# Taking the causal mask of transposed attention scores from TensorE to ScalarE and GpSimd

## The chip, the core and the metric

One NeuronCore of a Trainium2 chip runs the whole program. The metric is the device time of one execution in microseconds. The engines are named as the profile names them: PE (TensorE, matmuls and transposes; PEld is its weight load), DVE (VectorE), ACT (ScalarE), POOL (GpSimd), SP (SyncE, which issues most DMAs).

## The reference

Four layers run over x of 2048 rows and 512 columns: a spectral layer, an attention layer, and both again. The spectral layer adds to x the real part of a Fourier transform of its layernorm, as matrix products with given cosine and sine matrices. The attention layer has 32 heads of 16 columns and cuts the rows into 4 segments of 512:

```
for s in range(4):
    logits = einsum(qs, ks) * scale + mask          # scale = 16 ** -0.5
    p = softmax(logits)
    a_dot = einsum(p, vs)
    o = g * (phi(qs) @ M) / (phi(qs) @ z + 1e-6) + (1 - g) * a_dot
    M, z = M + phi(ks).T @ vs, z + sum(phi(ks))
```

The mask adds -1e9 where the key's index is greater than the query's within the segment. phi(t) is t + 1 above zero and exp(t) below; g is the sigmoid of beta, by head.

## The kernel before

The program is written as Python generators ("steps") that `place` puts into numbered slots; slots run in order, and inside a slot by a small order number. PE's instructions keep this order exactly. The instructions of the other engines are set in order by a scheduler, which looks at priorities and its own estimate of when operands are ready. PSUM has one bank for PV (`pv_bank`) and seven that every other matmul takes in turn (`bank`).

A spectral layer takes 240 slots and some lead. An attention layer takes 320: 32 units of 10 slots, each of 4 heads of one segment. The steps of a unit that begins at slot t:

- `stack` (t - 21) loads q and k of the unit from DRAM, three bf16 parts of each in 96 rows (tiles stkq, stkk).
- `natural_max` (t - 17 to t - 7): PE forms scores with queries in rows (tile nat, 10 banks a unit), DVE takes each row's maximum with the mask added (`junk`, L414, accumulator mx), and turns it into three bf16 parts of the negated maximum.
- `max_rows` (t - 5): PE transposes them (mT), ACT copies them (mt, L452) and issues a DMA that writes them as 3 more rows under q; k has ones there.
- `softmax_values` (t to t + 11): PE forms the transposed scores, keys in rows (tile sT, 99 rows, the maximum already subtracted), ACT takes Exp into tile pT, and PE multiplies with v (PV). For a key block kt only the query columns from kt * 128 on are formed. The ten banks of a unit are two `third` (blocks of 256 and 256 columns: key block 2 of two heads), four `second` (384 and 128: key blocks 1 and 3), four `first` (512: key block 0). They stand in slots t, t + 1; t + 2 to t + 5; t + 6 to t + 9. `last` (PV of all four heads, and the copy ot on ACT) stands in slot t + 11.
- `output` (t + 13): PE transposes ot (tile on), DVE divides by the softmax's sum, POOL adds the result to the memory's part in onat.

Only the first 128 columns of each block hold masked places, since there key and query come from the same 128 rows. They were masked by a second matmul into the same bank, of an identity and a constant tile mask_t:

```
T.matmul(ps[:, off : off + P], ident_b, mask_t, start=False, stop=True)
```

Beside the units run the projections (`proj`, tile pqk, for q and k of the next group; pvv for v), the layernorm of the next segment (`prep`: st, mv, r on POOL, xn), the output projection (on, oT, oh, po) and the memory (pm, pM, pkT). `proj` ends with ACT copying the bank to bf16 (parts 0), ACT making phi, DVE taking the remainder (rem), ACT rounding it (parts 1), POOL subtracting once more (parts 2, L347), and SP writing the parts to DRAM. Steps that fill a unit with matmuls go to `light` slots, which leave out two of ten: those of PV and of `output`.

Of the kernel before, what the change touches and what calls it, by code (L numbers as in the profile page):

```python
# [18 lines left out]
P = 128  # L19
# [11 lines left out]
LAST = range((NSEG - 1) * LT, NT)  # L31
EPS = 1e-5
SCALE = DH ** -0.5
MASK = -1e9 / SCALE
SLOTS = {"q": ((0, 3, 0), (1, 2, 0), (2, 1, 0)), "k": ((0, 3, 1), (0, 2, 1), (0, 1, 1))}
NSLOT = 6
KROWS = NSLOT * DH
# [8 lines left out]
def spectral_infini_kernel(  # L46
# [228 lines left out]
    def place_attention(x_in, x_out, t0, w_at, out_at, resident):  # L275
# [39 lines left out]
        def proj(s, g, n):  # L315
            ps = bank("pqk")
            for d in range(DT):
                matmul3(
                    ps,
                    lambda h: ws[n, d][:, h, g * P : (g + 1) * P],  # L320
                    lambda h: xT[s][:, h, d, :],
                    d == 0,
                    d == DT - 1,
                )
                if d + 1 < DT:
                    yield

            def phi_tile():
                if (s, g) not in phi:
                    phi[s, g] = pair("phi", "ut", 8, F32)  # L330
                return phi[s, g][:, "qk".index(n)]

            parts = sb.tile([P, 3, 512], BF16, name="parts", bufs=2)
            with_phi = (n == "q" and s > 0) or (n == "k" and s < NSEG - 1)
            late = s == 0 and g < 2
            rem = sb.tile([P, 512], F32, name="rem", bufs=1)
            A.activation(parts[:, 0], ps, AF.Copy)
            if with_phi:
                raw = sb.tile([P, 512], F32, name="praw", bufs=2)
                A.activation(raw, ps, AF.Copy if late else AF.Relu)  # L340
                if not late:
                    A.activation(phi_tile(), ps, AF.Exp)
            V.tensor_tensor(out=rem, in0=ps, in1=parts[:, 0], op=ALU.subtract)
            yield
            yield
            A.activation(parts[:, 1], rem, AF.Copy)
            G.tensor_tensor(out=parts[:, 2], in0=rem, in1=parts[:, 1], op=ALU.subtract)  # L347
            if with_phi and not late:
                V.scalar_tensor_tensor(
                    phi_tile(), phi_tile(), 1.0, raw, op0=ALU.min, op1=ALU.add  # L350
                )
            yield
            sd = dram.tile([NSLOT, P, 512], BF16, name=f"scr{n}", bufs=3)
            dst = sd.rearrange("o p s -> p o s")
            o = 0
            for a, cnt, step in SLOTS[n]:
                src = parts[:, a : a + cnt] if step else parts[:, a : a + 1].to_broadcast(
                    [P, cnt, 512]
                )
                nc.sync.dma_start(dst[:, o : o + cnt], src)  # L360
                o += cnt
            scr[s, g, n] = sd
            yield
            if with_phi and late:
                V.tensor_scalar_min(phi_tile(), raw, 0.0)
                A.activation(phi_tile(), phi_tile(), AF.Exp)
                V.scalar_tensor_tensor(
                    phi_tile(), raw, 0.0, phi_tile(), op0=ALU.max, op1=ALU.add
                )
                yield  # L370
# [21 lines left out]
        def natural_max(s, g, u):  # L392
            qs, ks = stacks[s, g, u, "q"], stacks[s, g, u, "k"]
            mx = sb.tile([P, HU, LT], F32, name="mx", bufs=2)

            def scores(*cols):
                ps = bank("nat")
                views, off = [], 0
                for h, i in cols:
                    n = (i + 1) * P  # L400
                    T.matmul(
                        ps[:, off : off + n],
                        qs[:KROWS, h, i * P : (i + 1) * P],
                        ks[:KROWS, h, :n],
                        start=True,
                        stop=True,
                    )
                    views.append((ps[:, off : off + n], mx[:, h, i : i + 1]))
                    off += n
                for src, dst in views:  # L410
                    n = src.shape[1]
                    junk = sb.tile([P, 512], BF16, name="junk", bufs=1)
                    with tc.high_priority(offset=URGENT):
                        V.tensor_tensor_reduce(  # L414
                            junk[:, :n], src, mask[:, 512 - n :], 1.0, -3e38,
                            ALU.add, ALU.max, dst,
                        )

            for h in range(HU):
                scores((h, 3))  # L420
                yield
                scores((h, 0), (h, 2))
                yield
                if h % 2:
                    scores((h - 1, 1), (h, 1))
                    yield
            parts = max_parts[((s * NG + g) * (HG // HU) + u) % 2]
            rem = sb.tile([P, HU, LT], F32, name="mrem", bufs=2)
            with tc.high_priority(offset=2 * URGENT):
                V.scalar_tensor_tensor(  # L430
                    parts[:, 0], mx, -2.0, mx, op0=ALU.mult, op1=ALU.add
                )
                for dst in rem, parts[:, 1]:
                    V.scalar_tensor_tensor(
                        dst, mx, -1.0, parts[:, 0], op0=ALU.mult, op1=ALU.subtract
                    )
                V.scalar_tensor_tensor(
                    parts[:, 2], rem, 1.0, parts[:, 1], op0=ALU.mult, op1=ALU.subtract
                )
            maxima[s, g, u] = parts  # L440
            yield
# [16 lines left out]
        def softmax_values(s, g, u):  # L458
# [3 lines left out]

            def scores(dst, *cols):
                ps = bank("sT")
                off = 0
                for h, kt in cols:
                    n = 512 - kt * P
                    T.matmul(
                        ps[:, off : off + n],
                        ks[:K, h, kt * P : (kt + 1) * P],  # L470
                        qs[:K, h, kt * P :],
                        start=True,
                        stop=False,
                    )
                    T.matmul(ps[:, off : off + P], ident_b, mask_t, start=False, stop=True)
                    off += n
                A.activation(dst, ps, AF.Exp, scale=SCALE)  # L477

            def pv(pv_bank, kt, pt, off):
                n = 512 - kt * P  # L480
# [16 lines left out]
            for h in range(HU):  # L497

                def first(h=h):
                    if h % 2 == 0:  # L500
                        p0.append(pair("pT", "wd", 8, F32))
                    scores(p0[h // 2][:, h % 2], (h, 0))

                ev(6 + h, first)
            for h in range(HU):

                def second(h=h):
                    if h % 2 == 0:
                        p1.append(pair("pT", "wd", 8, F32))
                    scores(p1[h // 2][:, h % 2], (h, 1), (h, 3))  # L510

                ev(2 + h, second)
            p2 = []
            for h in range(0, HU, 2):

                def third(h=h):
                    if h == 0:
                        p2.append(sb.tile([P, HU, 256], F32, name="pT2", tag="craw", bufs=2))
                    scores(p2[0][:, h : h + 2].rearrange("p h s -> p (h s)"), (h, 2), (h + 1, 2))

                ev(h // 2, third)

# [7 lines left out]
                A.activation(ot, pb, AF.Copy)  # L530
                outs[s, g, u] = ot

            ev(11, last)
            for t in range(12):
                for f in events.get(t, ()):
                    f()
                yield
# [183 lines left out]
            return n // USEG, n % USEG // NU, n % NU  # L721

        def light(t, n=SU):
            return [k for k in range(t, t + n) if (k - t0) % SU not in (1, 3)]

        def among(start, stop, n):
            at = light(start, stop - start)
# [8 lines left out]
            place(3, load_split(ws, (n, d), src, f"w{n}", "w", 16), [w_at(k) - 3, w_at(k)])  # L736
        for n in range(NSEG * USEG):
            t = t0 + SU * n
            place(0, softmax_values(*unit(n)), run_from(t, 12))
            place(1.9, output(*unit(n)), [t + 13])  # L740
            place(1.9, max_rows(*unit(n)), [t - 5])
            place(1, natural_max(*unit(n)), run_from(t - 17, 10), [t - 7])
            place(0.5, stack(*unit(n)), [t - 21])
# [65 lines left out]
        mids[2], out_tiles, b2, w_at(b2), lambda k: b2 + LB + 8 + k, {}  # L809
    )  # L810
    def setup():
        nonlocal ident, ident_b, mask, mask_t, same_head, gate
        with tc.issue_after(first_row[0].ins):
            ident = consts.tile([P, P], F32, name="ident")
            make_identity(nc, ident)
# [4 lines left out]
            G.affine_select(  # L820
                mask[:, 384:], mask[:, 384:], pattern=[[-1, P]], compare_op=ALU.is_ge,
                fill=MASK, base=0, channel_multiplier=1,
            )
            mask_t = consts.tile([P, P], BF16, name="mask_t")
            G.memset(mask_t, 0.0)
            G.affine_select(
                mask_t, mask_t, pattern=[[1, P]], compare_op=ALU.is_ge,
                fill=MASK, base=0, channel_multiplier=-1,
            )
            same_head = consts.tile([P, HG], F32, name="same_head")  # L830
            V.tensor_reduce(
# [14 lines left out]
            V.tensor_scalar(gate[:, 1], gate[:, 0], -1.0, 1.0, op0=ALU.mult, op1=ALU.add)  # L846
        yield

    ident = ident_b = mask = mask_t = same_head = gate = None
    place(5, setup(), [60])  # L850
    for t in sorted(slots):
        slots_done.append(t)
# [44 lines left out]
```

## Time and profile before

| | us |
|---|---|
| median of 3 runs | 1954.85 |
| lowest, highest | 1952.45, 1955.95 |
| the profiled execution | 1959.92 |
| its span | 1958.1 |
| PE busy | 1894.2 |
| DVE busy | 1104.0 |
| ACT busy | 799.2 |
| POOL busy | 214.4 |
| mask matmuls, 1024, as busy time of their own | 194.2 |

The span is the time from the first to the last instruction in the profiled execution. A row of the profile's groups names the source line, the engine, the operation, "out<-in" by tile, the shapes and the count; behind the bar stand the busy time, the mean duration in ns, and the idle time of the engine just before, with what ended it. Busy time of matmuls is modelled and neighbours overlap, so what a matmul costs PE is seen from one start to the next.

### The profile page before, as it was taken

What the parts mean: (1) busy time and instruction counts of PE and PEld (TensorE: products, weight loads), DVE (VectorE), ACT (ScalarE), POOL (GpSimd) and SP (SyncE); (2) the same over time, 40 slices, a digit from 0 to 9 for tenths busy, and PEclk for the clock granted to TensorE, in tenths of its full rate; (3) what the DMA queues carried; (4) which work ended last, traced back from release to release, by engine and by line L of the source; (5) the groups of instructions that cost most, each with busy time, mean ns of one, the idle gap of its engine ahead of it and who ended that gap; (6) DMA issues with size and microseconds to landing.
All of it is one profiled execution on the core that took longest, in us unless ns stands there. A gap on an engine that the chain in (4) does not pass through costs nothing.

```text
span 1958.1 us, 31336 instructions
## 1 busy us (share of the span) xinstructions
PE 1894.2 (97%) x11552; PEld 1393.7 (71%) x11552; DVE 1104.0 (56%) x3733; ACT 799.2 (41%) x1386; POOL 214.4 (11%) x280
## 2 busy tenths in 40 slices
PE   7999999999999999998899999999998999999998
PEld 5788888887556666665578888888875666666665
DVE  8522222255776877868744222222567768677684
ACT  3311212142655656455533121121426555565554
POOL 6100000011110111113110000000111101111110
PEclk9999999999999999999999999999999999999999
DMA  5423233345442434335234232323454434343331
GB/s 178 156 93 102 97 97 97 97 155 162 130 131 90 149 105 133 127 115 168 85 100 140 97 97 97 97 97 102 149 162 127 126 103 148 114 127 128 106 108 57
DMA packets 123113, 232.48 MB, mean 119 GB/s; under 512 B 14416, under 2 KB 63568, under 8 KB 122960
## 3 DMA queue, kind: packets, MB, share of 16 engines
q1 hardware_dynamic: 119696, 229.70, 36.4%
q8 instruction: 90, 1.47, 0.3%
q10 hardware_dynamic: 3264, 0.79, 0.2%
q14 instruction: 63, 0.52, 0.1%
HBM read 162.55 MB, written 67.11 MB: 117 GB/s over the span
## 4 chain that ended last, share of the span: by engine, by line
PE 74%; DVE 9%; issue 8%; DMA 5%; POOL 2%; ACT 1%; SPq 0%; POOLq 0%; DVEq 0%; ACTq 0%
PE u L71 33%; PE y L71 7%; PE sT L71 7%; PE pv_bank L71 5%; PE pqk L71 5%; PE nat L71 5%; DVE junk L414 4%; PE po L71 4%; PE pvv L71 3%; DMA xt<-mid 2%; DMA stkk<-scrk 2%; PE on L71 1%; DVE xn L143 1%; PE pM L71 1%; PE pm L71 1%
## 5 line engine op out<-in xcount | busy, mean ns | idle before, releaser
L71 PE MATMUL u<-chi,xh 128*128 128x512 f32 x2048 | 652.1, 392 | 14.3 <-DVE mv L124 9.0
L414 DVE CUSTOM_DVE_ANT_0 junk<-nat,mask 128x512 bf16<-128x512 f32 (+3 forms) x1024 | 498.0, 486 | 171.6 <-PE nat L71 146.8
L71 PEld LDWEIGHTS u<-chi,xh 128*128 128x128 f32 x2048 | 387.1, 189 | 97.5 <-ACT chi L83 9.0
L477 ACT ACTIVATE pT<-sT 128x512 f32<-128x512 f32 x640 | 368.6, 599 | 190.2 <-PE sT L71 180.5
L71 PE MATMUL u<-clo,xh 128*128 128x512 f32 x1024 | 401.1, 392 | 2.6 <-DVE clo L85 2.1
L85 DVE TENSOR_TENSOR clo<-craw,chi 128x1024 fp32r<-128x1024 f32 x124 | 153.0, 1234 | 423.2 <-ACT chi L83 422.8
L83 ACT ACTIVATE chi<-craw 128x1024 fp32r<-128x1024 f32 x124 | 131.3, 1059 | 533.0 <-PE u L71 523.6
L71 PE MATMUL sT<-stkq,stkk 99*128 99x256 bf16 (+3 forms) x1024 | 273.2, 307 | 7.8 <-DVE mx L414 5.9
L71 PE MATMUL nat<-stkk,stkq 96*128 96x512 bf16 (+3 forms) x1024 | 244.9, 300 | 19.5 <-DVE mx L414 7.6
L71 PEld LDWEIGHTS u<-clo,xh 128*128 128x128 f32 x1024 | 193.5, 189 | 43.2 <-DVE clo L85 3.5
L71 PEld LDWEIGHTS <-stkk 99*128 99x128 bf16 x1024 | 100.9, 99 | 140.0 <-issue 119.0
L71 PE MATMUL y<-wdt,ut 128*128 128x512 f32 x768 | 196.9, 390 | 0.0
L71 PE MATMUL sT<-mask_t,ident_b 128*128 128x128 bf16 x1024 | 194.2, 221 | 0.0
L71 PEld LDWEIGHTS y<-wdt,ut 128*128 128x128 f32 x768 | 144.1, 188 | 29.9
L71 PE MATMUL pv_bank<-pT,vt 128*17 128x256 f32 (+3 forms) x2048 | 160.2, 441 | 0.0
L128 POOL TENSOR_TENSOR r<-ve,half_neg 128x1 f32<-128x1 f32 x64 | 39.2, 614 | 920.5 <-DVE ve L126 904.9
L71 PEld LDWEIGHTS <-stkq 96*128 96x128 bf16 x1024 | 85.7, 98 | 62.3 <-issue 31.9
L71 PE MATMUL pqk<-xT,wq 128*128 128x512 f32 x384 | 125.6, 437 | 0.0
L71 PE MATMUL pqk<-xT,wk 128*128 128x512 f32 x384 | 125.4, 434 | 0.0
L71 PEld LDWEIGHTS pv_bank<-pT,vt 128*17 128x17 f32 x2048 | 61.7, 98 | 88.4 <-issue 80.4
L71 PE MATMUL pvv<-wv,xT 128*128 128x512 f32 x384 | 123.6, 430 | 0.0
L71 PE MATMUL po<-wo,oh 128*128 128x512 f32 x384 | 120.5, 429 | 1.1 <-ACT oh L83 0.7
(106 smaller groups left out, 1855.9 us busy)
## 6 DMA issues: line engine op xcount, KB each, us to landing
craw<-in_ct SPq DMA_DIRECT2D x124, 512.0 KB
stkq<-scrq SPq DMA_DIRECT2D x64, 384.0 KB
stkk<-scrk SPq DMA_DIRECT2D x64, 384.0 KB
mid<-xo SPq DMA_DIRECT2D x48, 256.0 KB
scrq<-parts SPq DMA_DIRECT2D x32, 384.0 KB
scrk<-parts SPq DMA_DIRECT2D x32, 384.0 KB
xr<-mid SPq DMA_DIRECT2D x48, 256.0 KB
xt<-mid SPq DMA_DIRECT2D x44, 256.0 KB
```

What stands on the lines that cost most here:

```text
L71: return tc.keep_in_program_order(op(*args, **kwargs))
L83: A.activation(hi, src, AF.Copy, scale=scale)
L85: lo_engine.tensor_tensor(out=lo, in0=src, in1=hi.bitcast(F32), op=ALU.subtract)
L128: G.tensor_tensor(out=r, in0=ve, in1=half_neg, op=ALU.pow)
L143: V.tensor_scalar(xn, xt, mv[:, 0:1], rr, op0=ALU.subtract, op1=ALU.mult)
L414: V.tensor_tensor_reduce(junk[:, :n], src, mask[:, 512 - n :], 1.0, -3e38, ALU.add, ALU.max, dst,)
L477: A.activation(dst, ps, AF.Exp, scale=SCALE)
```

## The change

The mask matmul and its tile mask_t go. q is negated when it is projected, so the scores in both forms are negated: the natural ones take a minimum with +1e9/scale added, and the transposed ones hold maximum minus score, which is not negative at any place that counts. On the diagonal blocks ACT applies Relu in place in PSUM, so that masked places, which may lie on the other side of zero, become zero and Exp of them stays at most 1; then Exp with -scale over the whole bank; then POOL's affine_select sets the masked half of the diagonal blocks in pT to zero. Selects are issued for two heads at once (`causal`): of `first` after heads 1 and 3, of `second` likewise for both blocks, of `third` once for four. `last` moves from slot t + 11 to t + 12, `output` from t + 13 to t + 14, and `light` leaves out slots 2 and 4 of ten where it left out 1 and 3.

```
-MASK = -1e9 / SCALE
+MASK = 1e9 / SCALE
...
-            A.activation(parts[:, 0], ps, AF.Copy)
+            sign = -1.0 if n == "q" else 1.0
+            A.activation(parts[:, 0], ps, AF.Copy, scale=sign)
...
-            V.tensor_tensor(out=rem, in0=ps, in1=parts[:, 0], op=ALU.subtract)
+            V.scalar_tensor_tensor(
+                rem, ps, sign, parts[:, 0], op0=ALU.mult, op1=ALU.subtract
+            )
...
-                            junk[:, :n], src, mask[:, 512 - n :], 1.0, -3e38,
-                            ALU.add, ALU.max, dst,
+                            junk[:, :n], src, mask[:, 512 - n :], 1.0, 3e38,
+                            ALU.add, ALU.min, dst,
...
                         start=True,
-                        stop=False,
+                        stop=True,
                     )
-                    T.matmul(ps[:, off : off + P], ident_b, mask_t, start=False, stop=True)
+                    diag.append(off // P)
                     off += n
-                A.activation(dst, ps, AF.Exp, scale=SCALE)
+                blocks = ps.rearrange("p (b c) -> p b c", c=P)
+                blocks = blocks[:, diag[0] : diag[-1] + 1 : max(1, diag[-1] - diag[0])]
+                A.activation(blocks, blocks, AF.Relu)
+                A.activation(dst, ps, AF.Exp, scale=-SCALE)
+
+            def causal(blocks):
+                G.affine_select(
+                    blocks,
+                    blocks,
+                    pattern=[[0, n] for n in blocks.shape[1:-1]] + [[1, P]],
+                    compare_op=ALU.is_ge,
+                    fill=0.0,
+                    base=0,
+                    channel_multiplier=-1,
+                )
...
+                    if h % 2:
+                        causal(p0[h // 2][:, :, :P])
...
+                    if h % 2:
+                        for c in 0, 3 * P:
+                            causal(p1[h // 2][:, :, c : c + P])
...
+                    if h == 2:
+                        causal(p2[0][:, :, :P])
...
-            ev(11, last)
-            for t in range(12):
+            ev(12, last)
+            for t in range(13):
...
-            return [k for k in range(t, t + n) if (k - t0) % SU not in (1, 3)]
+            return [k for k in range(t, t + n) if (k - t0) % SU not in (2, 4)]
...
-            place(0, softmax_values(*unit(n)), run_from(t, 12))
-            place(1.9, output(*unit(n)), [t + 13])
+            place(0, softmax_values(*unit(n)), run_from(t, 13))
+            place(1.9, output(*unit(n)), [t + 14])
```

The order of ACT's instructions (with the engines that each waits for) in the second attention layer, from the copy ot of one unit to the DMA of the maxima, before:

```order
L530 ACTIVATE ot<-pv_bank 128x512 [waits PE_49]
L346 ACTIVATE parts<-rem 128x512 [waits DVE_49]
L477 ACTIVATE pT_16940<-sT 128x512 [waits PE_49]
L477 ACTIVATE pT<-sT 128x512 [waits PE_49] x4
L452 ACTIVATE mt<-mT 48x128 [waits DMAHW0_49,PE_49]
L453 DMA stkq<-mt 3x16x128 [waits DMAHW0_49,Activation_49]
```

and after (L482 is the Relu, L483 the Exp):

```order
L482 ACTIVATE sT<-sT 128x2x128 [waits PE_49] x2
L483 ACTIVATE pT_16981<-sT 128x512 [waits Activation_49]
L349 ACTIVATE parts<-rem 128x512 [waits DVE_49]
L483 ACTIVATE pT_16981<-sT 128x512 [waits Activation_49]
L554 ACTIVATE ot<-pv_bank 128x512 [waits PE_49]
L482 ACTIVATE sT<-sT 128x2x128 [waits PE_49] x2
L483 ACTIVATE pT<-sT 128x512 [waits Activation_49] x2
L482 ACTIVATE sT<-sT 128x2x128 [waits PE_49]
L482 ACTIVATE sT<-sT 128x2x128 [waits DVE_49,PE_49]
L455 ACTIVATE mt<-mT 48x128 [waits DMAHW0_49,PE_49]
L483 ACTIVATE pT<-sT 128x512 [waits Activation_49] x2
L456 DMA stkq<-mt 3x16x128 [waits DMAHW0_49,Activation_49]
```

Each Exp now waits for its Relu instead of PE, and the Relu of the next bank often stands between the two.

PE's order in the same layer, around the transpose of the maxima mT (with what follows it in the next slot), before:

```order
L71 MATMUL mT<-ident_b,mparts_77 80x128
L71 MATMUL po<-wo,oh 128x512 x3
L71 LDWEIGHTS stkk
L71 MATMUL sT<-stkq,stkk 128x512 [waits Activation_49]
L71 LDWEIGHTS ident_b
L71 MATMUL sT<-mask_t,ident_b 128x128
L71 LDWEIGHTS stkq
L71 MATMUL nat<-stkk,stkq 128x128 [waits DVE_49]
```

and after:

```order
L71 MATMUL mT<-ident_b,mparts_77 80x128
L71 MATMUL po<-wo,oh 128x512 x3
L71 LDWEIGHTS stkk [waits PE_49]
L71 MATMUL sT<-stkq,stkk 128x512 [waits Activation_49]
L71 LDWEIGHTS stkq
L71 MATMUL nat<-stkk,stkq 128x128 [waits Activation_49]
L71 LDWEIGHTS stkq
L71 MATMUL nat<-stkk,stkq 128x384
```

The mask's weight load and matmul are gone, and nat, which waited for a bank that DVE frees, waits for one that ACT frees.

POOL's order in the same layer, one stretch of a unit or so, before it held only the subtraction, the adds and the layernorm's power; after:

```order
L486 AFFINE_SELECT pT<-pT 128x2x128 [waits PE_49,Activation_49,Pool_49]
L350 TENSOR_TENSOR parts<-rem,parts 128x512 [waits DMAHW3_49,DMAHW7_49,DMAHW2_49,Activation_49]
L486 AFFINE_SELECT pT<-pT 128x2x128 [waits PE_49,Activation_49,Pool_49]
L350 TENSOR_TENSOR parts<-rem,parts 128x512 [waits DMAHW6_49,DMAHW7_49,DMAHW5_49,Activation_49]
L486 AFFINE_SELECT pT_16981<-pT_16981 128x4x128 [waits PE_49,Activation_49]
```

Selects and subtractions alternate; each of both waits for ACT, the subtractions for earlier DMAs too.

More of the change, by code (lines that the diff above doesn't have):

```diff
@@ L464, in scores @@
                 ps = bank("sT")
-                off = 0
+                off, diag = 0, []
                 for h, kt in cols:
@@ L811, in setup @@
     def setup():
-        nonlocal ident, ident_b, mask, mask_t, same_head, gate
+        nonlocal ident, ident_b, mask, same_head, gate
         with tc.issue_after(first_row[0].ins):
@@ L822, in setup @@
                 fill=MASK, base=0, channel_multiplier=1,
[L823 to L828, printed above, removed]
             )
@@ L847, in setup @@
         yield
-    ident = ident_b = mask = mask_t = same_head = gate = None
+    ident = ident_b = mask = same_head = gate = None
     place(5, setup(), [60])
```

## The prediction

> **What bounds the kernel now.** I read the page's first part, then busy time by stretch, then one stretch instruction by instruction. The page gives
>
> ```profile
> PE 1894.2 (97%) x11552; PEld 1393.7 (71%) x11552; DVE 1104.0 (56%) x3733; ACT 799.2 (41%) x1386; POOL 214.4 (11%) x280
> ```
>
> and the view by stretch (columns: PE, weight load, DVE, ACT, POOL, granted clock, DMA share, GB/s) shows where the average hides something:
>
> ```profile
> 500.00:600.00 100.00, 92.65 (x739) 58.62 (x737) 71.52 (x301) 58.57 (x115) 11.25 (x11) 0.97 0.41 129
> ...
> 900.00:1000.00 100.00, 88.81 (x669) 55.20 (x667) 68.13 (x265) 51.70 (x94) 20.11 (x28) 0.93 0.35 116
> ...
> 1680.70:1697.50 16.80, 16.77 (x130) 11.54 (x133) 11.98 (x51) 10.94 (x22) 3.08 (x4) 1.00 0.42 134
> 1697.50:1712.00 14.50, 14.50 (x116) 9.21 (x115) 9.79 (x47) 7.10 (x14) 1.18 (x3) 1.00 0.22 70
> 1615.70:1633.20 17.50, 17.50 (x146) 13.13 (x149) 16.40 (x57) 10.60 (x21) 2.07 (x3) 1.00 0.52 167
> ```
>
> The last three are single attention units (from one PV group to the next, 64 in all): light, with a projection finished, and with a layernorm beside it. PE is busy to the last 0.03 us in all of them, so in a steady unit a PE nanosecond saved is a nanosecond of span. The first two rows hold the ramps into and out of attention, where PE idles 7 and 11 us: there it waits for others. What PE waits for elsewhere is small; its largest entry among the waits is
>
> ```profile
> PE mT L71 <- DVE mparts L437: 9.2, 5, 3.0
> ```
>
> Inside a steady unit (start, duration, instruction):
>
> ```profile
> 1708.13 0.39 PE L71 MATMUL sT<-stkq,stkk 99*128 99x512 bf16 x1
> ...
> 1709.34 0.39 PE L71 MATMUL sT<-stkq,stkk 99*128 99x512 bf16 x1
> 1709.57 0.22 PE L71 MATMUL sT<-mask_t,ident_b 128*128 128x128 bf16 x1
> 1709.63 0.38 PE L71 MATMUL nat<-stkk,stkq 96*128 96x128 bf16 x2
> 1710.55 0.28 PE L71 MATMUL sT<-stkq,stkk 99*128 99x256 bf16 x1
> 1710.68 0.22 PE L71 MATMUL sT<-mask_t,ident_b 128*128 128x128 bf16 x1
> 1710.74 0.27 PE L71 MATMUL sT<-stkq,stkk 99*128 99x256 bf16 x1
> ...
> 1711.99 0.61 PE L71 MATMUL pv_bank<-pT,vt 128*17 128x512 f32 x2
> ```
>
> Durations overlap, since matmuls are pipelined: the price of a mask matmul is not its 0.22 but the step to the next start, 0.06 us both times.
>
> **The change, part by part.** The rows for the prices:
>
> ```profile
> L71 PE MATMUL sT<-mask_t,ident_b 128*128 128x128 bf16 x1024 | 194.2, 221 | 0.0
> L477 ACT ACTIVATE pT<-sT 128x512 f32<-128x512 f32 x640 | 368.6, 599 | 190.2 <-PE sT L71 180.5 <-PE nat L71 5.8 <-ACT mt L452 1.6
> L452 ACT ACTIVATE mt<-mT 48x128 bf16<-48x128 bf16 x64 | 16.6, 260 | 21.4 <-PE mT L71 21.4
> L347 POOL TENSOR_TENSOR parts<-rem,parts 128x512 bf16<-128x512 f32 x64 | 77.4, 1209 | 334.7 <-ACT parts L346 283.6 <-DMA stkq<-scrq 33.6 <-issue 13.2
> masks.py:199 POOL TENSOR_SCALAR_AFFINE_SELECT ident<-ident 128x128 f32<-128x128 f32 x1 | 0.3, 287 | 0.0
> L819 POOL MEMSET mask<- 128x512 bf16 x1 | 0.5, 524 | 0.0
> L825 POOL MEMSET mask_t<- 128x128 bf16 x1 | 0.2, 204 | 0.0
> ```
>
> 1. *Mask matmuls gone.* 1024 x 0.06 = 61.4 us of PE, weight loads included (they ran beside the matmul before). Bounds: all of it in steady units, nothing where PE waits anyway. I put a quarter of the 64 units into the ramps and give those half: 61.4 - 7.7 = 53.7 us saved.
>
> 2. *Relu on ACT,* 256 on 128 columns and 384 on 256, in place in PSUM. No such row exists. Between 260 ns (128 columns) and 599 (512) the slope is 0.88 ns a column, so 0.26 and 0.37 us. Whether the Exp behind it must wait for its end decides the rest:
>
> ```profile
> 1705.35 0.26 ACT L452 ACTIVATE mt<-mT 48x128 bf16<-48x128 bf16 x1
> 1705.64 0.73 ACTq L453 DMA_DIRECT2D stkq<-mt  x1
> 1706.49 0.60 ACT L337 ACTIVATE parts<-pqk 128x512 bf16<-128x512 f32 x1 [0.88 <-PE nat L71]
> 1706.98 0.59 ACT L340 ACTIVATE praw<-pqk 128x512 f32<-128x512 f32 x1
> 1710.98 0.63 ACT L346 ACTIVATE parts<-rem 128x512 bf16<-128x512 f32 x1 [1.94 <-DVE rem L343]
> ```
>
> Independent ACT instructions overlap by 0.11 (0.60 long, next after 0.49). A dependent one starts after the end; the nearest rows for that are on DVE, three in a chain, 0.03 to 0.04 apart:
>
> ```profile
> 882.49 0.17 DVE L585 TENSOR_SCALAR den<-pm 128x16 f32<-128x16 f32 x1 [0.47 <-PE pm L71]
> 882.69 0.25 DVE L586 RECIPROCAL den<-den 128x16 f32<-128x16 f32 x1
> 882.98 0.17 DVE L587 TENSOR_TENSOR den<-den,gate 128x16 f32<-128x16 f32 x1
> ```
>
> So a Relu costs ACT 0.15/0.26 us when other work stands between it and its Exp (in the new order so for nearly three of four) and 0.30/0.41 when not: 138 to 234 us, 2.2 to 3.7 a unit. ACT with its DMA issue (0.73) fills 7.8 of the light unit and 11.7 of the projection unit; 11.5 of 13.5 and 15.4 of 15.8 after the change at the dear end. It fits, barely: the cover is gone in the projection units, and ACT answers PE later there. The price in time is that of item 5.
>
> 3. *Selects on POOL:* 384 of 256 and 64 of 512 elements. The two memsets give 0.83 ns an element, so 0.39 and 0.61 us; in steps of 287 ns per 128 it would be 0.57 and 1.15. That is 189 to 292 us, 3.0 to 4.6 a unit, beside at most 3.1 now: hidden as load. What queues behind a waiting select: the third parts (which feed the scratch DMAs), the adds into onat and the layernorm's power. And selects now queue behind those.
>
> 4. *DVE and constants.* The remainder becomes a three-operand op of the same length, the reduction takes the minimum; 0, no row speaks for another price (a dearer minimum would add 1024 times its excess to DVE). A constant less in the setup: 0, PE does not wait for POOL there.
>
> 5. *New waits.* (a) PV needs the select of the last p0 block. From the last 512-column sT to PV there were 1711.99 - 1709.34 = 2.65 us; PV one slot later makes it about 3.85 (a slot is 1709.34 - 1708.13 = 1.21). Needed: 0.39 sT, 0.26 + 0.04 Relu, 0.60 + 0.04 Exp, 0.39 to 0.57 select: 1.7 to 1.9. Covered by two microseconds, unless POOL holds a 1.21 subtract and another select ahead of it, or ACT stands at a rem (1.94 above). Between 0 and 1 us a unit; 0.1 taken, the slack being the nearest row: 6 us. (b) In the new order the nat behind mT waits for ACT where it waited for DVE: it takes over mT's bank. mt ended at 1705.61, that nat would start at about 1705.9; one Relu (0.37) ahead of mt uses the gap, a Relu and an Exp overrun it by 0.6. 0 to 0.6 a unit; 0.15 taken: 10 us. (c) The layernorm units, eight or so: DVE is at 16.40 of 17.50, PE could reach 16.54, no room; 0.25 each: 2 us. (d) At the two ends of attention little work is left to cover a slot more, the Relu (0.30) and the select (0.39):
>
> ```profile
> 1941.86 0.39 PE L71 MATMUL sT<-stkq,stkk 99*128 99x512 bf16 x1
> ...
> 1943.69 2.35 PE L71 MATMUL pv_bank<-pT,vt 128*17 128x512 f32 x32
> ```
>
> 0.7 to 3 us each; 2 taken: 4 us.
>
> 6. *Moved by a slot:* PV (32 PE rows) with its ot copy on ACT, and the output step (4 transposes, two small DVE ops, two products, two POOL adds); the projections change slots accordingly. No DMA is among them, so SP's queue keeps its order; what reads onat comes 20 and more slots later except at the ends, which (d) holds. The pT buffers stay in use a slot longer: the next unit's first write into them now falls into PV's own slot, but its sT stands behind PV on PE, so that Exp could not start sooner anyway. 0, and 0 to 0.3 us a unit if a release is late; in the range.
>
> One effect beside these: POOL's time is not free for DVE. The normalisation takes 643 ns on average and took 1.10 us while POOL subtracted:
>
> ```profile
> L143 DVE TENSOR_SCALAR xn<-xt,mv,rr 128x512 f32<-128x512 f32 x60 | 38.5, 643 | 6.9 <-PE xnT L71 3.6 <-POOL xh L85 1.7
> 1617.64 1.10 DVE L143 TENSOR_SCALAR xn<-xt,mv,rr 128x512 f32<-128x512 f32 x1
> 1617.30 1.16 POOL L347 TENSOR_TENSOR parts<-rem,parts 128x512 bf16<-128x512 f32 x1 [4.53 <-ACT parts L346]
> ```
>
> If twice as many of the some 32 in attention are hit, DVE works 4 us more, nearly all of it off the path (in (c)). The Trainium skill, GPSIMD Engine Reference, Specifications, says that GpSimd shares its SBUF interfaces with VectorE and gets in the way of DVE instructions in a two-port mode or with two SBUF inputs; the xn row agrees for the first kind. By the rule the DVE instructions with two SBUF inputs would be slowed as well, (c) would double, and the sum would be 2 us worse (an estimate).
>
> *Sum,* against the profiled execution (1959.9, span 1958.1): 1959.9 - 53.7 + 6 + 10 + 2 + 4 = 1928.2, 31.7 less. The median shown is 1954.85, 5.1 below that execution; the same 31.7 off the median gives 1923.
>
> **The rivals.**
> - *Everything is hidden.* At the cheap end ACT has 3.5 us to spare in light units (7.8 + 2.2 of 13.5). Then only the ramps count: 1954.85 - 61.4 to - 53.7, about 1897. Against it: ACT at 15.4 of 15.8.
> - *ACT's delay passes to PE through the banks.* Seven banks serve every matmul, and an sT bank is now held by two ACT instructions. If each unit loses two waits of 0.35 us (an unhidden Relu each), 64 x 0.7 = 45 on top of - 53.7 + 6: about 1952, no change. Decides: a Relu with its wait above (15.8 - 11.7)/10 = 0.41 us on average.
> - *Slower: PV waits for POOL.* POOL works in order; a select behind the parts subtract waits for that one's chain, rem on DVE (ACT stood 1.94 for it), ACT 0.63, POOL 1.21: 1.9 + 3.8 = 5.7 us needed against 3.85. If it lies so, 1.8 us a unit; at 1.2 on average 64 x 1.2 = 77 - 53.7, about 1978. It turns to a loss above 53.7/64 = 0.84 a unit. For it: POOL idled 283.6 us for ACT ahead of parts. Against it: that idling was mostly lack of work.
>
> **How the numbers follow.** Forecast as summed 0.57 (its own range 1905 to 1945), all hidden 0.12, banks 0.14, PV behind POOL 0.17. 0.2% is about what a measurement of this kernel can tell from no change, 1951 to 1958.8 here. Faster: 0.57 + 0.12 + 0.05 of the banks' case = 0.74; same 0.07; slower 0.17 + 0.02 = 0.19. The range from 1898 to 1964 leaves out the lower half of all hidden and most of the PV case above 1964.
>
> **What would show it.** Right: mask rows gone, light units near 13.6 us, PE still without idle time in them, ACT near 12 us of those, POOL's select below 0.6 us. Step 5a wrong: PV waiting for POOL among PE's waits; 5b: nat waiting for ACT mt; the banks: sT or nat waiting for ACT pT with tens of microseconds. Wrong as a whole if light units stay at 14.5, or if the Relu rows show over 0.41 us.

## The result and the profile after

| | us, median | beside before |
|---|---|---|
| before, four runs | 1954.18 (1952.45 to 1955.95) | |
| after, four runs | 1926.42 (1922.55 to 1928.27) | 0.9855 [0.9837, 0.9873] |

The change takes 27.8 us off the medians; 1923 was forecast (1898 to 1964). The profiled execution of after lies 4 us below its median (1922.55, span 1920.8), that of before nearly 6 us above its own, so the two traces differ by 37 us of which about 10 are spread. Comparisons below go by the medians and ratios; 0.001 of a ratio is 2 us. The engines of after, and its new rows (Relu is L482, Exp L483, select L486):

```profile
PE 1846.4 (96%) x10528; PEld 1330.6 (69%) x10528; DVE 1113.7 (58%) x3733; ACT 952.4 (50%) x2026; POOL 404.1 (21%) x726
```

```profile
L483 ACT ACTIVATE pT<-sT 128x512 f32<-128x512 f32 x640 | 366.8, 603 | 8.7 <-ACT sT L482 1.1
L482 ACT ACTIVATE sT<-sT 128x256 f32<-128x256 f32 x384 | 142.6, 386 | 26.9 <-PE sT L71 23.0 <-DVE mx L417 1.9 <-DVE state L657 0.3
L482 ACT ACTIVATE sT<-sT 128x128 f32<-128x128 f32 x256 | 65.3, 271 | 36.8 <-PE sT L71 34.7 <-ACT pT L483 1.3
...
L486 POOL TENSOR_SCALAR_AFFINE_SELECT pT<-pT 128x256 f32<-128x256 f32 x384 | 150.7, 408 | 369.2 <-ACT pT L483 218.3 <-issue 70.6 <-PE nat L71 43.0
L486 POOL TENSOR_SCALAR_AFFINE_SELECT pT<-pT 128x512 f32<-128x512 f32 x64 | 42.0, 656 | 89.7 <-ACT pT L483 87.4 <-DMA scrk<-parts 1.9
```

By stretch (columns: PE, weight load, DVE, ACT, POOL, clock, DMA share, GB/s): the hundred microseconds that the prediction counted as the ramp into attention, then a light, a projection and a layernorm unit:

```profile
500.00:600.00 100.00, 94.15 (x667) 57.19 (x659) 78.54 (x328) 76.73 (x186) 30.88 (x58) 0.97 0.38 121
...
1636.60:1651.13 14.53, 14.21 (x99) 8.31 (x98) 10.57 (x47) 9.63 (x24) 4.79 (x10) 1.00 0.35 107
1651.13:1667.22 16.09, 15.88 (x111) 10.18 (x111) 11.62 (x49) 13.23 (x33) 5.21 (x11) 1.00 0.44 148
1586.90:1603.70 16.80, 16.27 (x126) 11.65 (x127) 15.84 (x58) 12.60 (x30) 5.07 (x10) 1.00 0.52 167
```

The projection unit fell from 16.80 to 16.09 and the layernorm unit from 17.50 to 16.80, but the light one stands at 14.53 where it was 14.50 (from one first start of PV to the next, both are 14.53). There PE is idle for 0.3 us that it did not have before, and neither DVE (10.57) nor ACT (9.63) is full. What PE waits for (total, times, longest), after:

```profile
PE nat L71 <- DVE mx L417: 12.7, 25, 1.2
...
PE sT L71 <- DVE mx L417: 8.0, 25, 0.8
PE mT L71 <- DVE mparts L440: 7.5, 11, 2.5
PE mT L71 <- ACT pT L483: 3.7, 7, 0.6
```

The first two grew (7.6 and 5.9 us before); the third was 9.2. The list holds only idle time behind modelled durations; a wait that a modelled duration covers is not in it. So below, steps are used as well: from the start of one matmul of PE to the start of the next, added up over a whole trace by the tile that the later one writes.

### The profile page after: what moved, and what is told of

It is laid out like the page before. It is cut to its first block, busy times and chain, and to the rows that moved or that the text cites. A ratio compares the mean times of both kernels' runs of the same rounds, so it can differ in the third digit from the quotient of the medians.

```text
span 1920.8 us, 30840 instructions
## 1 busy us (share of the span) xinstructions
PE 1846.4 (96%) x10528; PEld 1330.6 (69%) x10528; DVE 1113.7 (58%) x3733; ACT 952.4 (50%) x2026; POOL 404.1 (21%) x726
## 4 chain that ended last, share of the span: by engine, by line
PE 73%; DVE 13%; issue 6%; ACT 4%; POOL 2%; DMA 2%; POOLq 0%; ACTq 0%; DVEq 0%; SPq 0%
PE u L71 34%; PE y L71 7%; DVE junk L417 6%; PE pv_bank L71 6%; PE pqk L71 6%; PE sT L71 5%; PE nat L71 5%; PE po L71 3%; PE pvv L71 3%; ACT pT L483 1%; DMA xt<-mid 1%; PE pM L71 1%; ACT sT L482 1%; PE pm L71 1%; POOL r L128 1%
## 5 line engine op out<-in xcount | busy, mean ns | idle before, releaser
L483 ACT ACTIVATE pT<-sT 128x512 f32<-128x512 f32 x640 | 366.8, 603 | 8.7 <-ACT sT L482 1.1
L486 POOL TENSOR_SCALAR_AFFINE_SELECT pT<-pT 128x256 f32<-128x256 f32 (+1 forms) x448 | 192.7, 443 | 458.9 <-ACT pT L483 305.6
L71 PE MATMUL sT<-stkq,stkk 99*128 99x256 bf16 (+3 forms) x1024 | 247.9, 306 | 12.0 <-DVE mx L417 8.0
L482 ACT ACTIVATE sT<-sT 128x256 f32<-128x256 f32 (+1 forms) x640 | 207.8, 340 | 63.7 <-PE sT L71 57.8
L71 PEld LDWEIGHTS <-stkk 99*128 99x128 bf16 x1024 | 83.3, 98 | 138.1 <-issue 125.0
L71 PE MATMUL pv_bank<-pT,vt 128*17 128x512 f32 (+3 forms) x2048 | 159.1, 439 | 0.1
L71 PEld LDWEIGHTS <-stkq 96*128 96x128 bf16 x1024 | 94.0, 98 | 79.0 <-issue 41.7
L71 PE MATMUL pqk<-xT,wq 128*128 128x512 f32 x384 | 129.6, 448 | 0.0
```

The lines of the kernel that those rows point to most:

```text
L71: return tc.keep_in_program_order(op(*args, **kwargs))
L482: A.activation(blocks, blocks, AF.Relu)
L483: A.activation(dst, ps, AF.Exp, scale=-SCALE)
L486: G.affine_select(blocks, blocks, pattern=[[0, n] for n in blocks.shape[1:-1]] + [[1, P]], compare_op=ALU.is_ge, fill=0.0, base=0, channel ...
```

## The experiments

All effects are differences of ratios to before, taken as microseconds of 1956.

**Parts of the change taken away.** c1 is before with this line gone (and the matmul ahead of it closing the sum); Exp's scale is divided by 64 so that unmasked scores stay finite, and the slots are those of before:

```
-                    T.matmul(ps[:, off : off + P], ident_b, mask_t, start=False, stop=True)
```

> The kernel before without its 1024 mask matmuls and with nothing in their place: no Relu, no select, slots as before. The scores stay unmasked, and Exp's scale is divided by 64 so that unmasked places stay finite. The change was forecast to save 53.7 to 61 us of PE and to give some 22 us back; measured is a gain of 28. Theory DVE (what PE saves it waits away for banks that DVE's maxima free, whatever replaces the mask): about as the changed kernel, 1918 to 1930. Theory ACT (the Relu holds the sT banks) and theory POOL (selects slow DVE and PV): the whole relief shows, 1893 to 1908.

Measured 1910.75, 0.9759 [0.9743, 0.9774]: 47 us, the ceiling, in these slots, for anything that takes the mask off PE and costs nothing. The steps from mask matmul to next start add up to 61. So 14 us do not arrive, and after pays 19 us for what stands in the mask's place.

Where the 14 go can be read from the two traces, since PE's order is the same but for the masks. The 1024 steps that held a mask are 60.6 us shorter in c1, as counted. All other steps together are 13.2 us longer, and 9.7 of that are steps to mT, the transpose of the maxima. PE's wait there, 9.2 us before, is in c1

```profile
PE mT L71 <- DVE mparts L437: 15.1, 18, 2.0
```

c2 is after without the Relus (Exp's scale by 64 again), c3 after without the 448 selects; both lack a part of the mask.

```
-                A.activation(blocks, blocks, AF.Relu)
```

> The changed kernel without the 640 Relus (Exp's scale divided by 64 so that masked places stay finite; the selects still set them to zero). Theory ACT: 15 to 30 us faster than the changed kernel, 1897 to 1912, since sT banks come free 0.3 to 0.4 us sooner. Theory DVE and theory POOL: within 6 us of it, 1920 to 1930.

```
-                        causal(p0[h // 2][:, :, :P])
...
-                            causal(p1[h // 2][:, :, c : c + P])
...
-                        causal(p2[0][:, :, :P])
```

> The changed kernel without the 448 selects on POOL (masked places keep weight 1). Theory POOL: 15 to 30 us faster, 1897 to 1912. Theory DVE and theory ACT: only what PE visibly waited for POOL, about 7 us in the trace, 1917 to 1926.

c2: 1913.56, 0.9777 [0.976, 0.9793]; c3: 1914.79, 0.9781 [0.9765, 0.9796]. Taking away either one gives 15 us back and leaves some 4 above the ceiling, with intervals that overlap c1's. The two prices do not add: one alone is nearly hidden, both together cost 19. All three times lie between the ranges of the theories, so none of the theories holds alone. PE's order in c2 and c3 is that of after, and the steps say where each price lies (the traces differ from after's by 9 and 11 us): without the Relus the steps to nat are 7.0 us shorter and those to sT 5.8; without the selects those to PV are 7.2 shorter and those to mT 3.5. (c2 and c3 stand in the later slots, c1 in those of before, so the move of a slot is in these differences too.)

c4 is after in the slots of before:

```
-            ev(12, last)
-            for t in range(13):
+            ev(11, last)
+            for t in range(12):
...
-            place(1.9, output(*unit(n)), [t + 14])
+            place(1.9, output(*unit(n)), [t + 13])
```

(`run_from` follows, and `light` leaves out 1 and 3 again.)

> The changed kernel with PV, output and the light slots put back to 11, 13 and (1, 3). By step 5a the slack before PV falls from 3.85 to 2.65 us against a need of 1.7 to 1.9, so most PVs are still covered: 0.1 to 0.3 us a unit more, 1930 to 1945. Rival: the slot is not needed, because PV's operands are early anyway: 1920 to 1930.

Measured 1946.05, 0.994 [0.9927, 0.9954], one microsecond above the range: the slot is worth 17 us, more than half of what the change gains. The wait that it covers is in c4's lists, a small part of it as idle time of PE's matmuls and most of it as idle time of the weight loads for PV:

```profile
PE pv_bank L71 <- POOL pT L486: 8.1, 17, 0.9
```

```profile
PEld pv_bank L71 <- POOL pT L486: 39.3, 51, 1.9
```

After has none of the first kind and 5.4 us of the second. The steps to PV add up to 185.3 us in c4 and to 153.8 in after, so 17 of 31 us arrive. Before with its PV a slot later was not run; what the move does without selects is not known.

**Is it VectorE that PE waits for?** The first reading of the traces (theory A) was that PE, now faster, stands behind the reductions of the maxima. d1, d2 and d3 take every maximum over half of the columns, in after, before and c1; Exp's scale is divided by 64. The maxima are not the true ones there.

```
-                    n = src.shape[1]
+                    n = src.shape[1] // 2
...
-                            junk[:, :n], src, mask[:, 512 - n :], 1.0, 3e38,
+                            junk[:, :n], src[:, :n], mask[:, 512 - 2 * n : 512 - n], 1.0, 3e38,
```

> The kernel after, but each row's extreme is taken over the first half of the columns only (VectorE does the same 1024 reductions on half the elements; the maxima are not the rows' true ones, so Exp's scale is divided by 64). PE's order is that of after. Theory A, PE waits for VectorE's reductions to free its banks: 20 to 35 us under after, 1890 to 1906. Theory B, what is left over comes from the series Relu, Exp, select ahead of PV: within 8 us of after, 1918 to 1930.

> The kernel before with the same halved reductions (Exp's scale divided by 64). Theory A: VectorE's waits were there already, partly covered by the mask matmuls: 8 to 25 us under before, 1930 to 1947. Theory B, PE was the only bound: within 6 us of before, over 1949.

> The kernel before without any mask (nothing in its place: the output is not the reference's) and with the halved reductions. The masks alone gave 47 of the 61 us that their steps add up to. Theory A, the other 14 were lost to waits for VectorE: 1885 to 1899. Theory B, PE's floor without masks is simply higher than the steps say: 1905 to 1912.

| | full reductions | halved | gain |
|---|---|---|---|
| before | 1 | 0.9878 [0.986, 0.9896], 1932.74 us | 24 us |
| after | 0.9855 | 0.9734 [0.9716, 0.9751], 1903.64 us | 24 us |
| without mask (c1) | 0.9759 | 0.9664 [0.9644, 0.9684], 1889.56 us | 19 us |

All three numbers fall where theory A put them, and still the table speaks against it as the explanation. PE does wait for VectorE, but as much before the change as after: the gain is 24, 24 and 19. With halved reductions the mask matmuls are worth 0.0214, 42 us, no more than with full ones, and after still pays 14 us over the kernel without masks (0.9734 to 0.9664). So VectorE's load does not account for the 14 us that do not arrive, and for at most 5 of the 19 that after pays. The missing time then lies in other waits: without masks and with halved reductions (d3) mT's wait is down to 5.6 us, but nat waits 10.9 for the load of stkk, against 6.4 with the masks (d2). The table corrects one thing: a unit in which PE shows no idle time can be bound by more than PE. From PV's first start to the next, before's projection unit falls from 16.76 to 16.17 us with halved reductions. Its light unit does not fall (14.53 to 14.64).

**How near is the edge?** e3 issues every Relu twice, e4 every select twice.

```
                 A.activation(blocks, blocks, AF.Relu)
+                A.activation(blocks, blocks, AF.Relu)
```

> The kernel after with each Relu issued twice (the second changes nothing; the whole reference is computed). Taking the Relus out gave 13 to 15 us. Theory A, a linear price of ACT's work ahead of Exp: 10 to 18 us over after, 1936 to 1945. Theory B, ACT near its end in units of 14.5 us: an sT bank is held 0.3 to 0.4 us longer ten times a unit and ACT has some 12 us of work, 25 to 50 us over after, 1951 to 1976. Theory C, only one of Relu and select counts, the longer path: under 5 us, up to 1931.

```
-                G.affine_select(
+                for _ in range(2):
+                    G.affine_select(
```

> The kernel after with each select issued twice (the whole reference is computed). Theory A, PV stands behind the last select: 0.41 us or more later in units without slack, 8 to 26 us over after, 1934 to 1952. Theory B, POOL's 3 us a unit more are beside other work and only VectorE's normalisation suffers: under 5 us, up to 1931.

e3: 2008.31 us, 1.0265 [1.025, 1.028]; 80 us over after, and beyond what any theory allowed. The first set of Relus cost 15, the second 80, or 1.25 us a unit for 2.1 us more of ACT's busy time (952 to 1089 us over 64 units). e4: 1937.74 us, 0.9902 [0.9886, 0.9919]; 9 us over after for 185 us more POOL work, in the range of the theory that PV stands behind the last select; its steps to PV grew by 8.4 us. So a longer stage on ACT stands at an edge, and one on POOL much less. In e3 no engine is full, in the hundred microseconds or in the light unit:

```profile
500.00:600.00 100.00, 88.23 (x608) 50.98 (x600) 70.85 (x287) 83.45 (x231) 28.22 (x53) 0.98 0.39 121
1700.40:1715.55 15.15, 14.43 (x99) 8.42 (x98) 10.37 (x47) 11.34 (x33) 4.54 (x9) 1.00 0.27 87
```

The edge is one of waiting, not of load. PE's order is that of after, and of the 82.6 us between the two traces 28.3 are in steps to sT, 24.8 in steps to PV and 13.9 in steps to nat. PV waits for the select again, whose chain the second Relu makes longer; its weight loads show it, where after has 5.4:

```profile
PEld pv_bank L71 <- POOL pT L487: 31.4, 43, 3.6
```

The steps to sT and nat hold waits of another kind. One place in e3, in order of time:

```profile
1759.64 0.62 PE L71 MATMUL pm<-state,phi 128*128 128x136 f32 x4
...
1760.11 0.38 PE L71 MATMUL sT<-stkq,stkk 99*128 99x512 bf16 x1
...
1760.31 0.17 DVE L610 TENSOR_SCALAR den<-pm 128x16 f32<-128x16 f32 x1 [0.47 <-PE pm L71]
1760.52 0.25 DVE L611 RECIPROCAL den<-den 128x16 f32<-128x16 f32 x1
...
1761.01 0.42 DVE L621 TENSOR_TENSOR onat<-pm,den 128x256 f32<-128x256 f32 x1
...
1761.49 0.39 PE L71 MATMUL nat<-stkk,stkq 96*128 96x128 bf16 x2 [1.01 <-DVE onat L621]
```

This nat started 1.38 us after the sT ahead of it: it takes over the bank of pm, which DVE frees last with onat. In after the same nat comes 0.22 us behind its sT, and its row names no wait:

```profile
1692.52 0.38 PE L71 MATMUL sT<-stkq,stkk 99*128 99x512 bf16 x1
...
1692.74 0.38 PE L71 MATMUL nat<-stkk,stkq 96*128 96x128 bf16 x2
```

The order of PE is the same in both, and DVE was given no more to do. In after the nat starts before DVE has read pm to the end, so it has another bank there. Which bank comes next, and in which order DVE and ACT work, is laid down when the program is built, from the scheduler's own estimates, and a longer ACT changes them. So a second Relu is paid for partly in waits for DVE and partly in waits of PV for POOL.

The light unit shows the same on a smaller scale. It took 14.53 us in after and in c2

```profile
1634.04:1647.78 13.74, 13.69 (x98) 8.36 (x97) 10.30 (x47) 7.67 (x16) 4.26 (x9) 1.00 0.35 115
```

with PE in the same order (13.94 in c1, 14.52 in c3, 14.06 in d1). The largest difference in it is the first sT of 256 columns. In after:

```profile
1648.17 0.69 DVE L344 SCALAR_TENSOR_TENSOR rem<-pqk,parts 128x512 f32<-128x512 f32 x1
1648.30 0.38 PE L71 MATMUL sT<-stkq,stkk 99*128 99x256 bf16 x2 [0.30 <-DVE mx L417]
...
1648.77 0.68 DVE L352 SCALAR_TENSOR_TENSOR phi<-phi,praw 128x512 f32<-128x512 f32 x1
...
1649.37 0.69 DVE L417 CUSTOM_DVE_ANT_0 junk<-nat,mask 128x512 bf16<-128x512 f32 x1
```

and in c2:

```profile
1645.17 0.39 PE L71 MATMUL sT<-stkq,stkk 99*128 99x256 bf16 x2
1645.48 0.69 DVE L344 SCALAR_TENSOR_TENSOR rem<-pqk,parts 128x512 f32<-128x512 f32 x1
1646.08 0.68 DVE L417 CUSTOM_DVE_ANT_0 junk<-nat,mask 128x512 bf16<-128x512 f32 x1
...
1646.69 0.69 DVE L352 SCALAR_TENSOR_TENSOR phi<-phi,praw 128x512 f32<-128x512 f32 x1
```

In c2 that sT does not stand behind DVE's last mx, and the reduction comes ahead of the sum for phi. So the light unit's 0.79 us are paid chiefly in waits for DVE, though ACT is idle for nearly five microseconds of it. They are not the Relu's alone: c1 has no Relu, and there the same sT stands behind the same mx:

```profile
1643.71 0.56 DVE L414 CUSTOM_DVE_ANT_0 junk<-nat,mask 128x384 bf16<-128x384 f32 x1
...
1644.19 0.69 DVE L343 TENSOR_TENSOR rem<-pqk,parts 128x512 f32<-128x512 f32 x1
1644.33 0.38 PE L71 MATMUL sT<-stkq,stkk 99*128 99x256 bf16 x2 [0.30 <-DVE mx L414]
```

In before DVE takes rem ahead of that reduction, and the sT waits for nothing:

```profile
1678.97 0.69 DVE L343 TENSOR_TENSOR rem<-pqk,parts 128x512 f32<-128x512 f32 x1
1679.26 0.28 PE L71 MATMUL sT<-stkq,stkk 99*128 99x256 bf16 x1
...
1679.58 0.55 DVE L414 CUSTOM_DVE_ANT_0 junk<-nat,mask 128x384 bf16<-128x384 f32 x1
```

The step to this sT takes 0.24 us in before and c2 and 0.69 in c1 and after. Nor is 0.79 the rule: of the ten light units of c2's trace four are 0.72 to 0.78 us shorter than in after, the other six 0.25 to 0.40.

**Other versions.** d4 puts PV and `output` one slot later still (13 and 15; `light` leaves out 3 and 5):

```
-            ev(12, last)
-            for t in range(13):
+            ev(13, last)
+            for t in range(14):
...
-            place(1.9, output(*unit(n)), [t + 14])
+            place(1.9, output(*unit(n)), [t + 15])
```

> The kernel after with PV, output and the slots that leave out other matmuls one slot later still (13, 15, and 3, 5 left out). The whole reference is computed. Theory A (VectorE): within 5 us of after, 1921 to 1931. Theory B (series delay ahead of PV): 6 to 15 us under after, 1911 to 1920.

1933.18, 0.9877 [0.9861, 0.9893], 4 us over after with overlapping intervals and above the ranges of both theories: the delay ahead of PV is not what is left. e6 issues the selects of key block 0 head by head:

```
-                    if h % 2:
-                        causal(p0[h // 2][:, :, :P])
+                    causal(p0[h // 2][:, h % 2, :P])
```

> The kernel after with the selects of key block 0 issued for each head (128 columns) rather than for two heads at once (the whole reference is computed). Theory A, PV waits for the last select: it ends 0.12 us sooner (287 against 408 ns) and the one before it sooner still, 3 to 8 us under after, 1918 to 1924. Theory B: within 2 us of after; POOL's 128 more instructions matter if it is over 1930.

1928.13, 0.9853 [0.9838, 0.9867]: no difference, which says the same from the other side. e5 masks key block 0 on PE again, keeps Relu and select for the other three, and stands in the slots of before:

```
-                        stop=True,
+                        stop=kt > 0,
                     )
+                    if kt == 0:
+                        T.matmul(ps[:, :P], ident_b, mask_t, start=False, stop=True)
...
+                if cols[0][1]:
+                    A.activation(blocks, blocks, AF.Relu)
```

> A mixture: key block 0 is masked by a matmul as before (256 of the 1024 masks), blocks 1 to 3 by Relu and select as after; PV and output in the slots of before. The whole reference is computed. Masks cost 47 us for 1024, so 12 for 256 over the 1911 without any: theory A, the select right ahead of PV is what costs, 1918 to 1926, no worse than after. Theory B, each Relu costs wherever it stands: 384 of 640 Relus at 15 us for all, 1927 to 1936.

1927.08, 0.9851 [0.9833, 0.9868], the same as after and on the line between the two theories, so it tells them apart no further. It does show what c4 waited for: in the same slots, with no select right ahead of PV, no wait of PV for POOL's selects is left, and the steps to PV add up to 156.3 us where c4 has 185.3. None of these beats after. Those that are faster lack a part of the mask or of the maxima; a way to keep Exp of the masked scores finite without a Relu was not tried.

## Why the prediction was right, step by step

The sum was -31.7 us and the medians gave -27.8. Its two halves were each a little too large: 53.7 saved and 22 given back, where 47 (c1) and 19 (after less c1) were measured. That the two errors, 7 and 3 us, nearly cancel is luck, and the 22 came near the 19 though the largest of its terms, the 10 us of (b), was not seen.

1. *Mask matmuls gone*, 53.7: 47. The price of a mask was right (60.6 us over 1024 steps); the failed part is "a PE nanosecond saved is a nanosecond of span", and with it "all of it in steady units". In the light unit c1 gains 0.60 us (14.53 to 13.94) where 16 x 0.06 = 0.96 were counted: its mask steps give 1.07 back, and one sT takes 0.45 more, behind a reduction that DVE now takes in another order. Over the whole trace 13.2 us come out in other steps, 9.7 of them at mT, which waits for DVE's parts of the maxima. Halving the reductions does not bring this time back (d2 and d3); what would stays open.
2. *Relu*, 0.26 and 0.37 us, took 0.271 and 0.386. "It fits, barely" was right for the whole and wrong on the place: the cover was said to be gone in the projection units, and it is the light units that gain nothing in after. ACT is at 9.63 of 14.53 there, 10.4 with its DMA issue, not near 12 of 13.6. "Wrong as a whole if light units stay at 14.5" came true: over the ten light units of the two traces the change lies between 0.18 us less and 0.14 more. The time held all the same because the gain lies in other units: 0.67 us in the projection unit (16.76 to 16.09), 0.64 in the layernorm unit (17.44 to 16.80), though only 0.13 in the unit ahead of that one. So the time was forecast better than the place it would come from, and that is in part luck.
3. *Selects* of 0.39 and 0.61 us took 0.408 and 0.656; the upper bounds (0.57 and 1.15) are out, and "below 0.6 us" held for the 384 but not for the 64.
4. *The minimum* costs what the maximum did: the 512-column reduction took 688 ns before and 687 after.
5. (a) The slack of 3.85 us is enough, and in c4, with 2.65, PV waits for POOL: the mechanism was right, and the 17 us that c4 pays are more than the 6 allowed, which were meant for the later slot. What (a) costs after the move is within the 9 to 15 us that selects cost in e4 and c3. (b) *nat behind mT waits for ACT's mt*, 10 us: not seen; no such wait is in the list. Its neighbour is, mT behind Exp, 3.7 us. (c) The layernorm units were given no gain ("no room") and 0.25 us of loss; the one shown gained 0.64. DVE's 16.40 fell to 15.84 in it, but its window in after holds one remainder fewer, which now falls into the unit ahead, so the cause stays open. (d) No loss of 2 us shows at the ends: the last PV group comes 12.19 us after the one ahead of it before, and 12.12 after, in the second layer; in the first 17.54 and 18.20, with 18.11 in c1, which has neither Relu nor select.
6. *The moved slot*, 0: the moved work costs less than it brings, and the move is worth 17.

The effect that was set beside these, POOL's time at DVE's expense, was put at 4 us off the path. DVE's busy time is 11 us less in c3 than in after (1102.6 to 1113.7), and it was not the normalisation, which took 643 ns on average again (621 in c3). The small steps that make the maxima's parts and the divisor are stretched; before, after and c3:

```profile
L430 DVE SCALAR_TENSOR_TENSOR mparts<-mx 128x16 bf16<-128x16 f32 x64 | 11.0, 172 | 0.9
L549 DVE TENSOR_TENSOR rec<-rec,gate 128x16 f32<-128x16 f32 x64 | 10.9, 171 | 0.1
```

```profile
L433 DVE SCALAR_TENSOR_TENSOR mparts<-mx 128x16 bf16<-128x16 f32 x64 | 15.8, 246 | 1.3
L573 DVE TENSOR_TENSOR rec<-rec,gate 128x16 f32<-128x16 f32 x64 | 14.0, 219 | 0.2
```

```profile
L433 DVE SCALAR_TENSOR_TENSOR mparts<-mx 128x16 bf16<-128x16 f32 x64 | 12.8, 200 | 1.3
L566 DVE TENSOR_TENSOR rec<-rec,gate 128x16 f32<-128x16 f32 x64 | 10.9, 171 | 0.2
```

Over the five kinds of these steps (four for the parts, one for the divisor) that is 54.7 us before, 68.3 after, 58.1 in c3: ten of the eleven microseconds. They stand in the chain from the maxima over mT and the DMA to the next sT. How much of the 15 us for the selects comes this way was not separated.

Of the rivals, *everything is hidden* is out (1897 would need the whole ceiling and more: 1911 is the floor for this), and *PV behind POOL* is what c4 shows at the old slots. *ACT's delay through the banks* is real, in the steps to nat and sT that c2 shortens and e3 lengthens: with twice the Relu a bank, e3 is slower than before. Its point of decision was 0.41 us on average, the wait included; the Relu alone is 0.32 in after (208 us over 640) and twice that in e3. Its price was put at 45 us; e3 pays 80, about half of it in steps to sT and nat and a quarter or more in PV behind POOL.

What stays open is why Relu and select cost some 4 us each alone, hardly clear of nothing, and 19 together. Orders of DVE and ACT and the hand-over of banks differ among all these builds, so that no two of them differ in one cost only.

## What to carry to other kernels

Take a cost away without putting anything in its place first: it gives the ceiling (here 47 of 61 us), and it shows how much the replacement may cost. Then double each replacement part; a part that costs 15 us once and 80 us twice stands at an edge, and the next change to that engine can fall off it though its busy share says 50%. When two builds run PE in the same order, lay their steps side by side: that showed where the lost 13 us lie, and the idle time of the weight loads showed 39 us of waiting where PE's own list had 8. When an operand gets one more stage, move its consumer by as much in the program's order: that one slot was worth 17 of the 28 us.

## What the runs showed of the hardware

POOL's select and some DVE instructions with two SBUF inputs do not run side by side: in the rows below the one that starts later ends later, by most of what is left of the other. In c2 phi's sum (0.68 us by itself) starts with 0.48 of a select left and takes 1.03, 0.35 more; in after it starts first, keeps its 0.68, and the select, with 0.41 of the sum left, takes 0.91 in place of 0.64:

```profile
503.49 0.64 POOL L482 TENSOR_SCALAR_AFFINE_SELECT pT<-pT 128x512 f32<-128x512 f32 x1 [1.60 <-ACT pT L479]
503.65 1.03 DVE L352 SCALAR_TENSOR_TENSOR phi<-phi,praw 128x512 f32<-128x512 f32 x1
```

```profile
501.52 0.68 DVE L352 SCALAR_TENSOR_TENSOR phi<-phi,praw 128x512 f32<-128x512 f32 x1
501.79 0.91 POOL L486 TENSOR_SCALAR_AFFINE_SELECT pT<-pT 128x512 f32<-128x512 f32 x1 [3.09 <-ACT pT L483]
```

A short DVE step can so last until the select ends, here to 1686.50 with the select ending at 1686.48:

```profile
1685.84 0.64 POOL L486 TENSOR_SCALAR_AFFINE_SELECT pT<-pT 128x512 f32<-128x512 f32 x1
...
1685.99 0.51 DVE L433 SCALAR_TENSOR_TENSOR mparts<-mx 128x16 bf16<-128x16 f32 x1
```

The Trainium skill's GPSIMD Engine Reference, Specifications, names this contention for two SBUF inputs; these rows agree. The prediction's 2 us by that rule counted the layernorm units alone; the rows show short steps stretched as well, by 10 us of DVE's busy time in all, and what they cost in time was not separated. That the normalisation belongs to the first kind there is inferred from its one tensor input; no row shows the mode. The reductions, which read PSUM and one SBUF operand, were not touched: 687 ns with POOL at 404 us of work, 688 with 214.
